# Converting float64 weights to float32 on the chip: a one-byte offset in the fetch, and four passes in another split over two engines

## The chip, the cores and the metric

The kernel runs on one core of a Trainium2 chip. The metric is the device time of one execution in microseconds (us). The core has five instruction streams: PE (TensorE, the matmuls; its weight loads are listed as PEld), DVE (VectorE), ACT (ScalarE), POOL (GpSimd) and SP (SyncE), which here only issues DMAs. Each stream runs its instructions in the order in which they were written and waits on semaphores for the others.

## The reference

The reference is an attention over 2 batches, 8 heads, 768 positions and head width 64, followed by two feed-forward layers on the 1536 x 512 result:

```python
scores = q @ k.T / 8 + bias(distance, head); scores masked to the last n_local and first n_global keys
x  = softmax(scores) @ v                      # float32, laid out as [1536, 512]
h  = x @ w_in;  x = (h * cos(h)) @ w_out      # w_in [512, 2048], w_out [2048, 512]
out = ((x @ w_a) * (x @ w_b)) @ w_out2        # w_a, w_b [512, 1536], w_out2 [1536, 512]
```

`q`, `k`, `v` are float32. The five weight matrices arrive as float64, and the chip's engines compute in float32, so the kernel turns the 64-bit words into float32 itself. A float64 word has a sign, 11 exponent bits and 52 mantissa bits; the float32 wanted has the same sign, 8 exponent bits and the upper 23 of the mantissa bits.

## The kernel before, in words

**Stages.** The attention comes first (`step`, the events table at the end of `tile_kernel`): twelve tiles of 128 queries, each cut into some forty steps (`TQ`, `S0`, `E0`, `T0`, `P0`, ...). A table gives each step a due time, and the steps are written in the order of those times; on PE, DVE, ACT and POOL that order is kept as written. Then comes `moe`: the first layer in three groups of 4, 6 and 6 blocks of 128 hidden columns, the second layer in six groups of 2 blocks. Each group goes over three chunks of 512 tokens. In this part only PE's order is kept as written; the order on the other engines is set by a scheduler when the program is built.

**A unit of the first layer** (`h_step`) is 12 matmuls into `h`, then on ACT a scaled copy `hs` (line 434), on DVE two passes that make the turns `u` (lines 435 and 436), on ACT the sine (line 440), on DVE the product (line 443), on ACT a rounded copy `gh` (line 455) and on POOL the rest `gl` (line 138). Pairs of `gh` and `gl` go into the 12 matmuls of `y` (lines 473 to 475), whose sum DVE adds to `yacc` (lines 477 and 479). Every matmul is done as three, with a rounded part and a rest of both operands.

**The weights** come in 68 blocks of 128 x 512 values, each 512 KB of float64. `load_block` fetches a block from SP's queue into a `raw` tile, of which there are two (the first six blocks go into the space of the accumulators). `conv_abs` and `conv_ops` make float32 of it: ACT takes the absolute value of the upper word as float32 (line 351, tile `cv`, two buffers), DVE clamps it (line 358), shifts it left by three (line 360), puts the sign and top exponent bit over it (line 361) and puts in three bits of the lower word (line 362). Then `conv_hi` rounds the block on ACT (`wh`, line 368) and `conv_lo` subtracts that on POOL (`wl`, line 138). Four blocks are converted during the attention, at the times of `CONV` and `OFF`; the others are converted in `moe`, where `fetch` writes each conversion ahead of the unit by whose turn it should be done.

Of the kernel before, what the change touches and what calls it, by code (L numbers as in the profile page):

```python
# [14 lines left out]
I32 = mybir.dt.int32  # L15
AF = mybir.ActivationFunctionType
# [3 lines left out]
P = 128  # L20
GLOB = 32
# [10 lines left out]
# When each step of a tile's attention is due, in tiles from the tile's own; the steps are written in the order of these.  # L32
# [3 lines left out]
OFF = (0.026, 0.448, 0.46, 1.374, 2.055, 2.1, 2.15)  # L36
# [11 lines left out]
def tile_kernel(ctx, tc, q, k, v, n_global, n_local, w_in, w_out, w_a, w_b, w_out2, out):  # L48
# [3 lines left out]
    DFF = w_in.shape[1]  # L52
    DF2 = w_a.shape[1]
# [33 lines left out]
    def read_counts():  # L87
        """The two int64 scalars as floats: high word (one more where the low word reads as negative) times 2^32, plus the low word."""
# [104 lines left out]
    def first_keys(i):  # L193
        """Keeps the first keys of a batch when its first tile has come."""
# [3 lines left out]
    def put_first_keys(i):  # L198
        """After the scores of tile i, the first keys of the batch take the place of its own first ones."""
# [3 lines left out]
    def split_v(i):  # L203
        """Three bfloat16 parts of V, the first with a column of ones beside it for the sum of the weights."""
# [92 lines left out]
    def first_values(i):  # L297
        """After the products of tile i with V, the first values of the batch take the place of its own first ones."""
# [28 lines left out]
    spare = [acc_pool.tile([P, 2, KD, 2 * P], I32, tag=f"acc{x}", name=f"raws{x}") for x in range(NCH)]  # L327

    def word_const(bits):
        return struct.unpack("<f", struct.pack("<I", bits))[0]  # L330

    def load_block(x):
        w, kind, idx = blocks[x]
        wi = w.bitcast(I32)
# [3 lines left out]
        else:  # L338
            raw = wp.tile([P, KD, 2 * P], I32, tag="raw", name=f"raw{x}", bufs=2)
        if kind == "col":  # L340
            nc.sync.dma_start(out=raw, in_=wi[:, idx * 2 * P:(idx + 1) * 2 * P].rearrange("(kk p) f -> p kk f", p=P))
        else:
            nc.sync.dma_start(out=raw, in_=wi[idx * P:(idx + 1) * P, :].rearrange("p (kk f) -> p kk f", kk=KD))
# [4 lines left out]
    def conv_abs(x):  # L348
        top = raws[x].rearrange("p k (f two) -> p k f two", two=2)[:, :, :, 1]
        cvs[x] = c = wp.tile([P, KD, P], I32, tag="cv", name=f"cv{x}", bufs=2)  # L350
        nc.scalar.activation(out=f(c), in_=f(top), func=AF.Abs)  # L351

    def conv_ops(x):
        pairs = raws.pop(x).rearrange("p k (f two) -> p k f two", two=2)
        low, top = pairs[:, :, :, 0], pairs[:, :, :, 1]
        c = cvs[x]
        return [
            lambda: nc.vector.tensor_scalar(out=f(c), in0=f(c), scalar1=word_const(896 << 20), scalar2=word_const((1151 << 20) - 1),  # L358
                                            op0=ALU.max, op1=ALU.min),
            lambda: nc.vector.tensor_scalar(out=c, in0=c, scalar1=3, scalar2=0x3FFFFFF8, op0=ALU.logical_shift_left, op1=ALU.bitwise_and),  # L360
            lambda: nc.vector.scalar_tensor_tensor(out=c, in0=top, scalar=-0x40000000, in1=c, op0=ALU.bitwise_and, op1=ALU.bitwise_or),  # L361
            lambda: nc.vector.scalar_tensor_tensor(out=c, in0=low, scalar=29, in1=c, op0=ALU.logical_shift_right, op1=ALU.bitwise_or)]  # L362
# [450 lines left out]
```

## Time and profile before

| | |
|---|---|
| timed runs | 732.21, 732.50, 733.02 us (median 732.5) |
| profiled execution, first to last instruction | 731.0 us |
| so around the span | 1.5 us |
| PE busy | 676.8 us (93%) |
| DVE busy | 510.7 us (70%) |
| ACT busy | 303.3 us (41%) |
| POOL busy | 289.8 us (40%) |
| DMA, all queues | 49.80 MB, 68 GB/s over the span |

The busy times are sums over stages that differ. The attention takes about the first 115 us, the first layer the next 300 and the second layer the rest. PE's busy time counts an instruction's whole stay in the pipeline, so the number of matmuls in a stretch tells more than the busy time. The granted clock is a share of 2.4 GHz.

### The profile page before, as it was taken

The page shows a single profiled execution, that of the slowest core. Times are in us where ns is not written, and L with a number is a line of the kernel's source. Part 1 is how long each engine was busy: PE and PEld are TensorE (multiplying, and loading weights), DVE is VectorE, ACT ScalarE, POOL GpSimd, SP SyncE. Part 2 cuts the span into 40 slices and gives each one's busy share as a digit, 9 for nine tenths or more (in the row PEclk, how much of TensorE's full clock was granted, in tenths as well). Part 3 has the DMA queues.
Part 4 walks back from the last instruction along what each step waited for, and adds up shares of the span by engine and source line. Part 5 has one row for each costly group of instructions (what it writes and reads, how often), then busy time and mean ns, then how long its engine had stood idle before and what let it go on. Part 6 is the DMA issues. An engine that isn't in the chain of part 4 may idle for free.

```text
span 731.0 us, 10359 instructions
## 1 busy us (share of the span) xinstructions
PE 676.8 (93%) x3936; PEld 556.5 (76%) x3936; DVE 510.7 (70%) x901; ACT 303.3 (41%) x559; POOL 289.8 (40%) x263
## 2 busy tenths in 40 slices
PE   4899998799885999999989698999999999999996
PEld 3778887588763788788878486888888888888885
DVE  6999898999999979859979715885727322222223
ACT  4798886554445444444454413334314111111110
POOL 5789851664444434425252404435315211111110
PEclk9999999989987799999999799999999999999998
DMA  9944320223333202201303101333301000000004
GB/s 210 249 108 107 81 48 1 86 71 103 98 103 115 87 30 87 87 1 58 105 11 109 64 0 31 106 114 95 117 1 57 1 1 0 1 1 0 1 29 150
DMA packets 65084, 49.80 MB, mean 68 GB/s; under 512 B 39168, under 2 KB 59648, under 8 KB 65024
## 3 DMA queue, kind: packets, MB, share of 16 engines
q1 hardware_dynamic: 65024, 49.04, 23.4%
q8 instruction: 33, 0.54, 0.3%
q14 instruction: 27, 0.22, 0.1%
HBM read 45.09 MB, written 3.15 MB: 66 GB/s over the span
## 4 chain that ended last, share of the span: by engine, by line
PE 50%; DVE 35%; ACT 6%; issue 4%; POOL 2%; DMA 2%; SPq 0%; POOLq 0%; ACTq 0%; DVEq 0%
DVE cv L361 6%; DVE u L436 5%; PE o L502 4%; PE o L503 4%; PE o L501 4%; DVE cv L362 4%; PE b L413 4%; PE b L412 4%; PE b L411 4%; PE a L412 4%; PE a L411 4%; PE a L413 4%; DVE u L435 4%; DVE cv L358 3%; DVE cv L360 3%
## 5 line engine op out<-in xcount | busy, mean ns | idle before, releaser
L138 POOL TENSOR_TENSOR wl<-cv,wh 128x512 fp32r<-128x512 f32 x68 | 97.1, 1431 | 167.1 <-ACT wh L368 163.9
L138 POOL TENSOR_TENSOR glu<-as,ghu 128x512 fp32r<-128x512 f32 x36 | 47.5, 1320 | 158.5 <-ACT ghu L455 158.5
L491 DVE TENSOR_TENSOR as<-b,as 128x512 f32<-128x512 f32 x36 | 24.8, 689 | 117.6 <-PE b L413 116.4
L138 POOL TENSOR_TENSOR gl<-u,gh 128x512 fp32r<-128x512 f32 x48 | 69.8, 1464 | 74.4 <-ACT gh L455 62.3
L411 PE MATMUL h<-xTh,wh 128*128 128x512 f32 x192 | 79.1, 412 | 7.6 <-ACT hs L434 5.8
L473 PE MATMUL y<-gh,wh 128*128 128x512 f32 x192 | 75.4, 393 | 9.2 <-ACT gh L455 9.2
L474 PE MATMUL y<-gl,wh 128*128 128x512 f32 x192 | 76.0, 396 | 6.4 <-POOL gl L138 6.4
L412 PE MATMUL h<-xTl,wh 128*128 128x512 f32 x192 | 79.0, 411 | 0.0
L413 PE MATMUL h<-xTh,wl 128*128 128x512 f32 x192 | 78.6, 409 | 0.0
L475 PE MATMUL y<-gh,wl 128*128 128x512 f32 x192 | 75.2, 392 | 0.0
L368 ACT ACTIVATE wh<-cv 128x512 fp32r<-128x512 f32 x68 | 42.7, 628 | 69.1 <-DVE cv L362 58.2
L440 ACT ACTIVATE u<-u,quarter 128x512 f32<-128x512 f32 x48 | 34.7, 723 | 72.1 <-DVE u L436 72.1
L507 DVE TENSOR_TENSOR oacc<-o,oacc 128x512 f32<-128x512 f32 x60 | 41.2, 690 | 31.6 <-PE o L503 31.6
L411 PE MATMUL a<-yh,wh 128*128 128x512 f32 x144 | 57.2, 398 | 6.3 <-ACT as L488 4.2
L411 PE MATMUL b<-yh,wh 128*128 128x512 f32 x144 | 57.6, 400 | 3.0 <-ACT hs L434 3.0
L488 ACT ACTIVATE as<-a 128x512 f32<-128x512 f32 x36 | 21.4, 593 | 88.6 <-PE a L413 88.6
L361 DVE SCALAR_TENSOR_TENSOR cv<-raw,cv 128x512 int32<-128x512 int32 x62 | 57.4, 926 | 0.9
L412 PE MATMUL a<-yl,wh 128*128 128x512 f32 x144 | 57.1, 396 | 0.6 <-DVE yl L482 0.6
L413 PE MATMUL b<-yh,wl 128*128 128x512 f32 x144 | 57.4, 398 | 0.0
L412 PE MATMUL b<-yl,wh 128*128 128x512 f32 x144 | 57.2, 398 | 0.0
L413 PE MATMUL a<-yh,wl 128*128 128x512 f32 x144 | 57.0, 396 | 0.0
L351 ACT ACTIVATE cv<-raw 128x512 f32<-128x512 f32 x62 | 41.4, 668 | 37.2 <-POOL wl L138 18.0
(106 smaller groups left out, 1540.7 us busy)
## 6 DMA issues: line engine op xcount, KB each, us to landing
raw<-in_moe_w_out_dram SPq DMA_DIRECT2D x26, 512.0 KB, 3.3
raw<-in_moe_w_in_dram SPq DMA_DIRECT2D x12, 512.0 KB, 3.7
raw<-in_moe_w_a_dram SPq DMA_DIRECT2D x12, 512.0 KB, 3.6
raw<-in_moe_w_b_dram SPq DMA_DIRECT2D x12, 512.0 KB, 3.6
nv<-in_v_dram SPq DMA_DIRECT2D x12, 256.0 KB, 4.3
out_dram<-oacc SPq DMA_DIRECT2D x12, 256.0 KB, 2.9
nq<-in_q_dram SPq DMA_DIRECT2D x11, 256.0 KB, 3.6
nk<-in_k_dram SPq DMA_DIRECT2D x11, 256.0 KB, 4.4
```

Of the source, the lines that this page charges most:

```text
L138: nc.gpsimd.tensor_tensor(out=dst, in0=a, in1=b, op=ALU.subtract)
L351: nc.scalar.activation(out=f(c), in_=f(top), func=AF.Abs)
L361: lambda: nc.vector.scalar_tensor_tensor(out=c, in0=top, scalar=-0x40000000, in1=c, op0=ALU.bitwise_and, op1=ALU.bitwise_or),
L368: nc.scalar.activation(out=hi, in_=f(cvs[x]), func=AF.Copy)
L411: nc.tensor.matmul(dst, wh[:, kk, :], xh[:, kk, :], start=(kk == 0), stop=False)
L412: nc.tensor.matmul(dst, wh[:, kk, :], xl[:, kk, :], start=False, stop=False)
L413: nc.tensor.matmul(dst, wl[:, kk, :], xh[:, kk, :], start=False, stop=(kk == KD - 1))
L436: nc.vector.scalar_tensor_tensor(out=u, in0=u, scalar=MAGIC, in1=hs, op0=ALU.subtract, op1=ALU.subtract)
L473: nc.tensor.matmul(yps, wh[:, m, :], gh, start=(x == 0), stop=False)
L474: nc.tensor.matmul(yps, wh[:, m, :], gl, start=False, stop=False)
L475: nc.tensor.matmul(yps, wl[:, m, :], gh, start=False, stop=(x == len(items) - 1))
L507: nc.vector.tensor_tensor(out=acc[:, u, :], in0=ops, in1=acc[:, u, :], op=ALU.add)
```

## The change

The host lays `w_in`, `w_a` and `w_b` out by blocks, so that each block is one piece of memory with 4 KB for each partition; the values and bytes stay the same. Every block is now fetched as bytes to an address one byte further on in the `raw` tile. The tile's 32-bit words are then no longer the lower and upper halves of a value: the word that is read holds the lower four exponent bits and the upper mantissa bits, and the byte with the sign and the upper seven exponent bits is read by itself, as a signed byte. ACT makes two float32 tiles of that byte, `cv` = relu(2^27 byte - 56 2^27) and `cn` = relu(-2^27 byte - 56 2^27), where `low_end` holds the second term, one value for each partition. DVE subtracts the two and writes the difference as an integer, which has the sign and the top exponent bits in place; a second DVE pass shifts the word right by five and puts it in. `cn` has one buffer. The second and third columns of times in `OFF` are now those of the two DVE passes; those of the former third and fourth passes are gone. The changes not shown remove docstrings and two unused names.

```diff
 P = 128
+RAW_BYTES = 8 * 4 * P + 32
+TOP = float(2.0**27)
-OFF = (0.026, 0.448, 0.46, 1.374, 2.055, 2.1, 2.15)
+OFF = (0.026, 0.448, 0.46, 2.1, 2.15)
...
-    spare = [acc_pool.tile([P, 2, KD, 2 * P], I32, tag=f"acc{x}", name=f"raws{x}") for x in range(NCH)]
+    spare = [acc_pool.tile([P, 2, RAW_BYTES], U8, tag=f"acc{x}", name=f"raws{x}") for x in range(NCH)]
+    low_end = const.tile([P, 1], F32, tag="lowend", name="low_end")
+    nc.gpsimd.memset(low_end, -56.0 * TOP)
...
-            raw = wp.tile([P, KD, 2 * P], I32, tag="raw", name=f"raw{x}", bufs=2)
-        if kind == "col":
-            nc.sync.dma_start(out=raw, in_=wi[:, idx * 2 * P:(idx + 1) * 2 * P].rearrange("(kk p) f -> p kk f", p=P))
-        else:
-            nc.sync.dma_start(out=raw, in_=wi[idx * P:(idx + 1) * P, :].rearrange("p (kk f) -> p kk f", kk=KD))
+            raw = wp.tile([P, RAW_BYTES], U8, tag="raw", name=f"raw{x}", bufs=2)
+        block = w[idx] if kind == "col" else w[idx * P:(idx + 1) * P, :]
+        nc.sync.dma_start(out=raw[:, 1:1 + 8 * KD * P], in_=block.bitcast(U8))
...
     def conv_abs(x):
-        top = raws[x].rearrange("p k (f two) -> p k f two", two=2)[:, :, :, 1]
-        cvs[x] = c = wp.tile([P, KD, P], I32, tag="cv", name=f"cv{x}", bufs=2)
-        nc.scalar.activation(out=f(c), in_=f(top), func=AF.Abs)
+        top = raws[x].bitcast(I8)[:, 8:8 + 8 * KD * P].rearrange("p (k f e) -> p k f e", k=KD, e=8)[:, :, :, 0]
+        cvs[x] = c, n = [wp.tile([P, KD, P], F32, tag=t, name=f"{t}{x}", bufs=b) for t, b in (("cv", 2), ("cn", 1))]
+        nc.scalar.activation(out=c, in_=top, func=AF.Relu, bias=low_end, scale=TOP)
+        nc.scalar.activation(out=n, in_=top, func=AF.Relu, bias=low_end, scale=-TOP)
 
     def conv_ops(x):
-        pairs = raws.pop(x).rearrange("p k (f two) -> p k f two", two=2)
-        low, top = pairs[:, :, :, 0], pairs[:, :, :, 1]
-        c = cvs[x]
+        words = raws.pop(x).bitcast(I32)[:, 0:2 * KD * P].rearrange("p (k f two) -> p k f two", k=KD, two=2)[:, :, :, 1]
+        c, n = cvs[x]
+        ci = c.bitcast(I32)
         return [
-            lambda: nc.vector.tensor_scalar(out=f(c), in0=f(c), scalar1=word_const(896 << 20), scalar2=word_const((1151 << 20) - 1),
-                                            op0=ALU.max, op1=ALU.min),
-            lambda: nc.vector.tensor_scalar(out=c, in0=c, scalar1=3, scalar2=0x3FFFFFF8, op0=ALU.logical_shift_left, op1=ALU.bitwise_and),
-            lambda: nc.vector.scalar_tensor_tensor(out=c, in0=top, scalar=-0x40000000, in1=c, op0=ALU.bitwise_and, op1=ALU.bitwise_or),
-            lambda: nc.vector.scalar_tensor_tensor(out=c, in0=low, scalar=29, in1=c, op0=ALU.logical_shift_right, op1=ALU.bitwise_or)]
+            lambda: nc.vector.tensor_tensor(out=ci, in0=c, in1=n, op=ALU.subtract),
+            lambda: nc.vector.scalar_tensor_tensor(out=ci, in0=words, scalar=5, in1=ci, op0=ALU.logical_shift_right, op1=ALU.bitwise_or)]
...
-        for y, fn in enumerate((conv_abs, conv_op, conv_op, conv_op, conv_op, conv_hi, conv_lo)):
+        for y, fn in enumerate((conv_abs, conv_op, conv_op, conv_hi, conv_lo)):
...
-        a = _np.ascontiguousarray(inputs[name])
+        a = inputs[name]
+        if name in ("moe_w_in", "moe2_w_a", "moe2_w_b"):
+            a = a.reshape(a.shape[0] // P, P, a.shape[1] // P, P).transpose(2, 1, 0, 3)
+        a = _np.ascontiguousarray(a)
```

The change also moves instructions, since the scheduler orders the engines other than PE anew. On DVE, around the second unit of the first layer's second group (`u0_1_1`; `cv19` is the tile of weight block 19), stood before:

```order
L443 SCALAR_TENSOR_TENSOR u0_1_0_3144<-hs0_1_0_3143,u0_1_0_3144 128x512
L358 TENSOR_SCALAR cv19_3082<-cv19_3082 128x512
L360 TENSOR_SCALAR cv19_3082<-cv19_3082 128x512
L361 SCALAR_TENSOR_TENSOR cv19_3082<-raw19_3017,cv19_3082 128x512
L435 TENSOR_SCALAR u0_1_1_3194<-hs0_1_1_3193 128x512
L362 SCALAR_TENSOR_TENSOR cv19_3082<-raw19_3017,cv19_3082 128x512
L436 SCALAR_TENSOR_TENSOR u0_1_1_3194<-u0_1_1_3194,hs0_1_1_3193 128x512
L477 COPY yacc1_3065<-y1_0_3_3204 128x512
L358 TENSOR_SCALAR cv20_3170<-cv20_3170 128x512
L443 SCALAR_TENSOR_TENSOR u0_1_1_3194<-hs0_1_1_3193,u0_1_1_3194 128x512
```

Now the same unit on DVE reads:

```order
L440 SCALAR_TENSOR_TENSOR u0_1_0_3146<-hs0_1_0_3145,u0_1_0_3146 128x512
L358 TENSOR_TENSOR cv20_3172<-cv20_3172,cn20_3173 128x512
L359 SCALAR_TENSOR_TENSOR cv20_3172<-raw20_3021,cv20_3172 128x512
L358 TENSOR_TENSOR cv21_3222<-cv21_3222,cn21_3223 128x512
L359 SCALAR_TENSOR_TENSOR cv21_3222<-raw21_3082,cv21_3222 128x512
L432 TENSOR_SCALAR u0_1_1_3196<-hs0_1_1_3195 128x512
L433 SCALAR_TENSOR_TENSOR u0_1_1_3196<-u0_1_1_3196,hs0_1_1_3195 128x512
L474 COPY yacc1_3067<-y1_0_3_3206 128x512
L440 SCALAR_TENSOR_TENSOR u0_1_1_3196<-hs0_1_1_3195,u0_1_1_3196 128x512
```

Blocks 20 and 21 now stand whole ahead of this unit, where block 19 was in work before. On ACT, around the same unit's `hs0_1_1`, stood before:

```order
L440 ACTIVATE u0_1_0_3144<-u0_1_0_3144,quarter_94 128x512
L351 ACTIVATE cv19_3082<-raw19_3017 128x512
L368 ACTIVATE wh18_3037<-cv18_3031 128x512
L434 ACTIVATE hs0_1_1_3193<-h0_1_1_3180 128x512
L455 ACTIVATE gh0_1_0_3150<-u0_1_0_3144 128x512
L368 ACTIVATE wh19_3088<-cv19_3082 128x512
```

Now ACT has there:

```order
L437 ACTIVATE u0_1_0_3146<-u0_1_0_3146,quarter_94 128x512
L351 ACTIVATE cn20_3173<-raw20_3021,low_end_112 128x512
L350 ACTIVATE cv21_3222<-raw21_3082,low_end_112 128x512
L351 ACTIVATE cn21_3223<-raw21_3082,low_end_112 128x512
L365 ACTIVATE wh20_3178<-cv20_3172 128x512
L431 ACTIVATE hs0_1_1_3195<-h0_1_1_3182 128x512
L452 ACTIVATE gh0_1_0_3152<-u0_1_0_3146 128x512
L365 ACTIVATE wh21_3228<-cv21_3222 128x512
L437 ACTIVATE u0_1_1_3196<-u0_1_1_3196,quarter_94 128x512
```

`hs0_1_1` now stands behind the passes of two blocks; `cn21` needs the one `cn` buffer, which DVE's subtraction for block 20 gives back. In the attention the two DVE passes of a block stand at the places of the former first two; for block 0 the place of the former third and fourth passes was this:

```order
L191 TENSOR_TENSOR kx_81<-tk1_0_203,kx_81 128x512
L361 SCALAR_TENSOR_TENSOR cv0_227<-raws0_109,cv0_227 128x512
L266 TENSOR_TENSOR pt0_0_1_243<-tp0_0_1_242,pt0_0_1_243 128x2x128
L362 SCALAR_TENSOR_TENSOR cv0_227<-raws0_109,cv0_227 128x512
L684 TENSOR_TENSOR su_104<-su_104 128x256
```

In the attention the rest of the order on DVE is as it was, with the `cv` rows of the third and fourth passes taken out.

## Rows read from the trace of the kernel before

**Rows 1.** Chain of work that ended last, shares of the span by engine and line
```profile
PE 50%; DVE 35%; ACT 6%; issue 4%; POOL 2%; DMA 2%; SPq 0%; POOLq 0%; ACTq 0%; DVEq 0%
DVE cv L361 6%; DVE u L436 5%; PE o L502 4%; PE o L503 4%; PE o L501 4%; DVE cv L362 4%; PE b L413 4%; PE b L412 4%; PE b L411 4%; PE a L412 4%; PE a L411 4%; PE a L413 4%; DVE u L435 4%; DVE cv L358 3%; DVE cv L360 3%
```

**Rows 2.** Stretches: us; PE, PEld, DVE, ACT, POOL busy (instructions); clock; DMA share; GB/s
```profile
15.00:60.00 45.00, 38.66 (x561) 32.86 (x562) 44.55 (x134) 34.29 (x77) 36.27 (x42) 1.00 0.70 174
115.00:246.00 131.00, 110.27 (x427) 86.95 (x427) 128.07 (x176) 65.52 (x109) 63.48 (x43) 0.88 0.27 85
246.00:300.00 54.00, 54.00 (x240) 44.70 (x239) 48.29 (x63) 25.22 (x43) 22.11 (x17) 1.00 0.22 69
300.00:402.00 102.00, 99.48 (x437) 81.53 (x436) 83.95 (x115) 45.06 (x76) 38.73 (x28) 1.00 0.20 61
402.00:450.00 48.00, 40.39 (x158) 32.05 (x156) 22.75 (x31) 15.21 (x26) 15.08 (x12) 0.89 0.08 25
450.00:727.00 277.00, 272.12 (x1191) 224.69 (x1191) 123.86 (x184) 63.35 (x104) 69.50 (x53) 0.99 0.14 46
```

**Rows 3.** PE's waits, 115 to 246 us: total us, times, longest us
```profile
PE y L473 <- ACT gh L455: 8.0, 3, 3.5
PE h L411 <- ACT hs L434: 5.8, 2, 3.0
PE y L474 <- POOL gl L138: 5.1, 4, 1.9
PE h L411 <- DVE xTl L320: 1.9, 1, 1.9
```

**Rows 4.** DVE in the first layer: start us, duration us, product of each unit
```profile
221.20 0.68 DVE L443 SCALAR_TENSOR_TENSOR u<-hs,u 128x512 f32<-128x512 f32 x1
...
228.43 0.68 DVE L443 SCALAR_TENSOR_TENSOR u<-hs,u 128x512 f32<-128x512 f32 x1
...
235.74 1.23 DVE L443 SCALAR_TENSOR_TENSOR u<-hs,u 128x512 f32<-128x512 f32 x1 [0.19 <-ACT u L440]
```

**Rows 5.** Tile cv alone: us; DVE, ACT, POOL busy (instructions); clock; DMA share; GB/s
```profile
15.00:60.00 45.00, 10.15 (x11) 3.27 (x5) 4.15 (x3) 1.00 0.70 174
115.00:246.00 131.00, 76.08 (x96) 30.80 (x49) 35.37 (x24) 0.88 0.27 85
```

**Rows 6.** Tile cv: count, shortest/median/longest ns, first and last start, forms
```profile
L358 DVE TENSOR_SCALAR cv<-cv x68: 411/422/1521, 13.6 to 562.6; 128x512 f32<-128x512 f32 x68
L360 DVE TENSOR_SCALAR cv<-cv x68: 408/427/1511, 14.0 to 563.5; 128x512 int32<-128x512 int32 x68
L368 ACT ACTIVATE wh<-cv x68: 612/632/637, 18.6 to 566.4; 128x512 fp32r<-128x512 f32 x68
...
L351 ACT ACTIVATE cv<-raw x62: 643/668/694, 123.2 to 561.1; 128x512 f32<-128x512 f32 x62
L361 DVE SCALAR_TENSOR_TENSOR cv<-raw,cv x62: 675/691/1807, 126.9 to 564.0; 128x512 int32<-128x512 int32 x62
L362 DVE SCALAR_TENSOR_TENSOR cv<-raw,cv x62: 675/684/1779, 127.8 to 564.7; 128x512 int32<-128x512 int32 x62
```

**Rows 7.** Groups by line and form: busy us, mean ns, idle before
```profile
L361 DVE SCALAR_TENSOR_TENSOR cv<-raw,cv 128x512 int32<-128x512 int32 x62 | 57.4, 926 | 0.9
L362 DVE SCALAR_TENSOR_TENSOR cv<-raw,cv 128x512 int32<-128x512 int32 x62 | 53.2, 858 | 0.8
...
L440 ACT ACTIVATE u<-u,quarter 128x512 f32<-128x512 f32 x48 | 34.7, 723 | 72.1 <-DVE u L436 72.1
```

**Rows 8.** PE's waits, 402 to 455 us: total us, times, longest us
```profile
PE a L411 <- ACT as L488: 4.2, 1, 4.2
PE b L411 <- ACT hs L434: 3.0, 1, 3.0
```

**Rows 9.** DMA issues: count, KB each, median us to landing
```profile
raw<-in_moe_w_out_dram SPq DMA_DIRECT2D x26, 512.0 KB, 3.3
raw<-in_moe_w_in_dram SPq DMA_DIRECT2D x12, 512.0 KB, 3.7
...
nk<-in_k_dram SPq DMA_DIRECT2D x11, 256.0 KB, 4.4
```

More of the change, by code (lines that the diff above doesn't have):

```diff
@@ L1 @@
 import math
-import struct
 from contextlib import ExitStack
@@ L15 @@
 I32 = mybir.dt.int32
+U8 = mybir.dt.uint8
+I8 = mybir.dt.int8
 AF = mybir.ActivationFunctionType
@@ L51, in tile_kernel @@
     NT, DM = out.shape
-    DFF = w_in.shape[1]
-    DF2 = w_a.shape[1]
     KD = DM // P
@@ L326, in tile_kernel @@
     seen = set()
-    spare = [acc_pool.tile([P, 2, KD, 2 * P], I32, tag=f"acc{x}", name=f"raws{x}") for x in range(NCH)]
-    def word_const(bits):
-        return struct.unpack("<f", struct.pack("<I", bits))[0]
+    spare = [acc_pool.tile([P, 2, RAW_BYTES], U8, tag=f"acc{x}", name=f"raws{x}") for x in range(NCH)]
+    low_end = const.tile([P, 1], F32, tag="lowend", name="low_end")
+    nc.gpsimd.memset(low_end, -56.0 * TOP)
     def load_block(x):
         w, kind, idx = blocks[x]
-        wi = w.bitcast(I32)
         if x < 2 * NCH and x not in seen:
@@ L367, in conv_hi @@
         lo = pool.tile([P, KD, P], F32R, tag="wl", name=f"wl{x}", bufs=bufs)
-        nc.scalar.activation(out=hi, in_=f(cvs[x]), func=AF.Copy)
+        nc.scalar.activation(out=hi, in_=cvs[x][0], func=AF.Copy)
         ready[x] = (hi, lo)
@@ L372, in conv_lo @@
         hi, lo = ready[x]
-        pool_sub(lo, f(cvs.pop(x)), f(hi))
+        pool_sub(lo, cvs.pop(x)[0], f(hi))
     def convert_block(x):
```

## The prediction

> **What bounds the kernel now.** I read the chain of waits first: VectorE (DVE) holds 35% of it, and the four passes of the weight conversion, lines 358, 360, 361 and 362, are 3 + 3 + 6 + 4 = 16% of the span [rows 1]. A share of a chain is no saving, so I went to the table of stretches [rows 2]. From 246 to 300 us TensorE (PE) does 240 matmuls in 54.0 us at the full clock: 0.225 us for each, PE's own pace. Against that pace 115 to 246 us needs 427 x 0.225 = 96.1 us and takes 131, so 34.9 us are lost; 300 to 402 loses 102 - 437 x 0.225 = 3.7; 402 to 450 loses 48 - 35.6 = 12.4; 450 to 727 loses 277 - 268 = 9.0. The largest loss lies where DVE is busy for 128.07 of 131 us, while ScalarE (ACT) has 65.52 and GpSimd (POOL) 63.48 [rows 2]. PE there waits for `gh`, `hs` and `gl`, 20.8 us in four kinds of wait [rows 3], and each comes from a queue that waits for DVE. The granted clock averages 0.88 in that stretch: the matmuls after such a pause run at 1.2 GHz before 2.4 comes back, which is the rest of the loss. At its worst a unit takes (235.74 - 221.20) / 2 = 7.27 us [rows 4], against 24 x 0.225 = 5.4 us of matmuls. In the attention, 15 to 60 us is a second stretch with a full DVE, 44.55 of 45 us; PE has 38.66 [rows 2].
>
> **What the change takes from DVE.** From 115 to 246 us DVE makes 96 passes on `cv`, 24 blocks, in 76.08 us, 3.17 us a block [rows 5]. The medians of the four passes sum to 0.422 + 0.427 + 0.691 + 0.684 = 2.22 us; the longest ones are 1.5 to 1.8 [rows 6], so about 0.95 us a block is waiting inside the instruction. The trace has a POOL subtraction of each block beside these passes, 35.37 us in the same stretch [rows 5], and I take that for what they wait for.
>
> The new block has a subtraction of two tiles and a shift with an or. The second is the form of line 362. The first, float32 in and integers out, stands nowhere in the trace: its bounds are 0.42, the pass over one tile, and 1.38 us, two passes of the kind of line 361 [rows 6]; I take line 361, the nearest in form, since it too reads two tiles. So a block costs 0.691 + 0.684 = 1.375 us undisturbed, or 0.926 + 0.858 = 1.784 at the means [rows 7]. If the collisions all stay, the relief is 24 x (2.22 - 1.375) = 20.3 us; if they go with the passes, 76.08 - 24 x 1.784 = 33.3 us. Both ends are below the 34.9 that PE lost, so PE's own pace is not reached before DVE's relief is used up.
>
> **What it adds to ACT.** One pass of 0.668 us becomes two with a bias for each partition. Such a pass stands in the trace as the sine, 0.723 us [rows 7]; the read with gaps costs 0.668 - 0.632 = 0.036 over a plain copy [rows 6]; together 0.76, with bounds of 0.63 (the copy) and, since no row reads bytes, 1.34 (twice the present pass). At 0.76 that is 2 x 0.76 - 0.668 = 0.85 us a block, and 24 x 0.85 = 20.4 us in the stretch: ACT goes from 65.5 to 86 us of busy time, which has room in 131 us, and in 111 too. At 1.34 it would be 65.5 + 24 x 2.01 = 114, and ACT's case below would hold.
>
> Room is not all, since ACT works in order. The second new pass waits for the single `cn` buffer, which DVE's subtraction for the block before gives back; behind it stand `wh` and `hs0_1_1`, as the new order of ACT shows, and `hs` is what DVE's next unit and a free `h` bank for PE wait for. So a unit with two blocks becomes a round through both queues: on DVE the product (0.69), the subtraction and the or (1.375), then, once `hs` is there, the first two passes of the next unit (0.42 + 0.69, medians of rows 6 for the same forms), on ACT `wh` and `hs` (0.63 each) and the sine (0.72). That is 5.16 us, and with one collision (1.8 - 0.69 = 1.1) 6.3 us. Against 7.27 it is 13% less, or 17 us of 131.
>
> Three estimates of the gain from 115 to 246 us: 17 by the round, 20.3 and 33.3 by DVE's work. I take 20, near the two lower ones.
>
> The Trainium skill speaks against moving this work at all: in ScalarE: Activation LUTs, Rules for kernel authors, relu, max and min belong on VectorE and not on ScalarE, being up to three times faster there (it says so of bf16). The trace agrees as far as it goes, 0.42 us for the clamp on DVE against 0.67 us for an ACT pass [rows 6]. By that rule nothing is won, 0.85 us off DVE for 0.85 us onto ACT in a block; it decides if ACT becomes the engine that is waited for, the first of the other ways below.
>
> **The attention.** From 15 to 60 us DVE makes 11 conversion passes, 2.75 blocks, in 10.15 us [rows 5]. At 1.375 to 1.784 us a block the relief is between 2.75 x 0.85 = 2.3 and 10.15 - 2.75 x 1.784 = 5.2 us; DVE is full there, so it shows. ACT gets 2.75 x 0.85 = 2.3 us on 34.29 of 45, which hides it. I take 3 us. What is late next is PE, at 38.66 of 45.
>
> **Elsewhere.** From 246 to 402 us DVE is relieved as well, but PE already loses only 3.7 us. From 402 to 450 us it loses 12.4 us with DVE at 22.75 of 48 [rows 2]: PE waits for ACT's `as` and `hs` in the change from the first to the second layer [rows 8], a chain that goes back and forth between engines, in which a conversion loses 0.85 us on DVE and gains 0.85 on ACT. I count it at 0, with 6 us either way. POOL's `wl` and ACT's `wh` stay as they are.
>
> **The fetch.** A block lands 3.3 to 3.7 us after its issue [rows 9]. Blocks from `w_in`, `w_a` and `w_b` come in longer pieces than before, so 3.3 is the lower bound. A write to an odd address has no row. The dearest row nearby is the load of `k`, 256 KB in 4.4 us [rows 9], so twice that, 8.8 us, bounds a block from above. I take the near end, 3.5: the size and the queue are those of the 3.3 row. The issue stays one DMA a block, in the background with DMA at 27% [rows 2].
>
> **Sum.** 731.0 - 20 - 3 = 708.0 us of span. The timed median, 732.5, lies 1.5 us over the span of the profiled execution; with that, 709.5 us.
>
> **The other ways.**
>
> ACT takes over. For it: each of its waits lies in the same round, and the new one comes on top. Against it: DVE's backlog is what most of its idle time waits for. If half of the 65.5 us in which ACT now stands idle stays, the stretch needs 86 + 33 = 119 us, a gain of 12; with 2 in the attention and 1 lost at the change of layers, 719.5 us. Chance 0.17.
>
> The whole loss comes back. For it: conversions stand earlier in the new order (blocks 20 and 21 done ahead of the unit that had block 19), so the second half of the stretch finds them made. The relief of 30, 4 in the attention, and 6 of the 12.4 us at the change of layers make 40: 692.5 us. Chance 0.19.
>
> The conversion becomes no cheaper. With the subtraction at 1.38 us and the collisions kept, 0.16 us a block is left of the 0.85, 4 us; the longer ACT round eats it: 732 us. Chance 0.03.
>
> Slower: odd addresses make the fetch the bound. With two `raw` buffers, a buffer's round is the landing, two ACT passes (1.5) and two DVE passes (1.4). A block is needed every 131 / 24 = 5.5 us, a buffer every 10.9, so it decides from a landing of 8.0 us on. At 8.8 a block takes 5.85 us, the stretch 140, 9 more than now. The first eight blocks come while the attention loads its tiles with DMA at 70% [rows 2]: 8 x 5.5 us more, less the idle 30% of 45 us, is 30 us late. Sum about 770 us. Against it: nothing in the trace; for it: nothing either, hence a chance of 0.06.
>
> **How the numbers follow.** My forecast, 709.5, has 0.55, with its own range of 699 to 716. The range over the cases runs from 690, which takes in most of the full recovery, to 726, which takes in ACT as the bound; outside lie the fetch, the dear conversion and the tails. 0.2% is 1.5 us, about what a measurement of this kernel can tell from no change. Faster by more: 0.55 + 0.17 + 0.19, less 0.01 for a tail of ACT's case, 0.90. Within: 0.03. Slower: the fetch at 0.06 and 0.01 of that tail, 0.07.
>
> **What would show it.** Right: `cv` has two DVE passes of some 0.69 us at the median, from 115 to 240 us DVE falls below 90% busy, the number of matmuls in 20 us rises to about 80, the waits for `gh` and `hs` shrink, and ACT has 20 us more work there. The attention ends some 3 us sooner. ACT's case would show as PE waiting for `hs` behind `cn` waits with DVE idle. Wrong altogether: landings of `raw` over 8 us, or a subtraction over 1.3 us at the median.

## The result, and the profile after

The changed kernel takes **715.0 us** (median of 4 runs, 713.97 to 716.69) against 732.76 (4 runs, 732.21 to 733.1) of the kernel before: ratio 0.9751, 95% interval 0.9734 to 0.9768, a gain of 17.8 us. Its profiled execution is 712.9 us, 18.1 less than the 731.0 of before. The forecast was 709.5 us, a gain of 23.

The lines that answer to the rows of before have other numbers now: the two relus are 350 (`cv`) and 351 (`cn`), DVE's subtraction is 358 and its shift with or 359, `wh` is 365, POOL's subtractions are 139, `hs` is 431, the product is 440, `gh` is 452. The chain of waits, shares by engine and by line [rows 1]:

```profile
PE 61%; DVE 18%; ACT 8%; POOL 5%; issue 5%; DMA 2%; DVEq 0%; POOLq 0%; ACTq 0%; SPq 0%
PE o L500 5%; PE o L499 5%; PE o L498 5%; PE b L408 4%; PE b L409 4%; PE b L410 4%; PE a L409 4%; PE a L410 4%; PE a L408 4%; DVE cv L358 3%; DVE cv L359 3%; DVE u L433 3%; DVE u L432 3%; PE o L281 3%; PE y L471 3%
```

DVE has halved its share, the conversion's 16% are 6. The same stretches as in [rows 2], with the same columns (us; PE, PEld, DVE, ACT, POOL busy; clock; DMA share; GB/s):

```profile
15.00:60.00 45.00, 39.63 (x553) 33.51 (x552) 41.56 (x127) 36.05 (x82) 34.12 (x42) 0.96 0.66 169
115.00:246.00 131.00, 118.17 (x483) 94.63 (x482) 114.08 (x142) 88.58 (x144) 65.44 (x45) 0.93 0.30 97
246.00:300.00 54.00, 54.00 (x240) 44.66 (x239) 40.87 (x50) 29.96 (x50) 23.39 (x17) 1.00 0.19 59
402.00:450.00 48.00, 44.62 (x182) 35.97 (x181) 19.36 (x23) 16.60 (x27) 14.00 (x11) 0.93 0.14 44
```

In 115 to 246 us PE does 483 matmuls where it did 427; DVE is 87% busy, ACT has 23 us more. PE's waits there, total us, times and longest [rows 3]:

```profile
PE y L471 <- POOL gl L139: 4.1, 3, 2.0
PE h L408 <- ACT hs L431: 3.7, 2, 3.2
PE h L408 <- DVE xTl L321: 3.6, 1, 3.6
PE y L470 <- ACT gh L452: 1.5, 2, 1.1
```

The waits for `gh` and `hs` went from 13.8 to 5.2 us, all four kinds together from 20.8 to 12.9. DVE, which before waited 1.8 us in all from 113 to 246 us, now waits 16.3, most of it for `cn`:

```profile
DVE cv L358 <- ACT cn L351: 9.2, 11, 2.1
```

Tile `cv` alone, DVE, ACT and POOL busy [rows 5], and its durations, with those of `cn` (shortest/median/longest ns) [rows 6]:

```profile
15.00:60.00 45.00, 4.29 (x5) 3.44 (x5) 3.29 (x3) 0.96 0.66 169
115.00:246.00 131.00, 53.67 (x53) 34.38 (x50) 36.69 (x25) 0.93 0.30 97
```

```profile
L358 DVE TENSOR_TENSOR cv<-cv,cn x68: 674/693/1787, 13.6 to 545.0; 128x512 int32<-128x512 f32 x68
...
L350 ACT ACTIVATE cv<-raw,low_end x62: 741/758/780, 121.0 to 543.3; 128x512 f32<-128x512 int8 x62
L359 DVE SCALAR_TENSOR_TENSOR cv<-raw,cv x62: 674/693/1784, 125.8 to 545.7; 128x512 int32<-128x512 int32 x62
```

```profile
L351 ACT ACTIVATE cn<-raw,low_end x62: 730/750/785, 123.2 to 544.0; 128x512 f32<-128x512 int8 x62
```

The means, with busy time, mean ns and the idle time before [rows 7], and the landings of the blocks [rows 9]:

```profile
L358 DVE TENSOR_TENSOR cv<-cv,cn 128x512 int32<-128x512 f32 x68 | 65.7, 966 | 29.1 <-ACT cn L351 25.0
...
L359 DVE SCALAR_TENSOR_TENSOR cv<-raw,cv 128x512 int32<-128x512 int32 x62 | 61.5, 993 | 1.2
```

```profile
raw<-in_moe_w_out_dram SPq DMA_DIRECT2D x26, 512.0 KB, 3.3
raw<-in_moe_w_in_dram SPq DMA_DIRECT2D x12, 512.0 KB, 3.3
```

Over the whole run, the DVE passes on `cv` beside which no two-input pass of POOL runs (67) take 674 to 782 ns, and the other passes on `cv` (69) take 1255 ns on average. So POOL is what the passes wait for, as the prediction took it.

**Where the time went.** PE does the same 2448 matmuls of 128x512 in the two layers, in the same order. Counted by their starts in the trace, these are the stretches of work (us), here and in the runs told of below. "First" is the start of the first of them, a matmul of `h`; "to 432" is the time from there until 432 of them have started, and so on; "last" is the last of the 2448. Each ratio is to the kernel before as it was timed together with that run:

| run | first | to 432 | to 1080 | to 1296 | to last | median of runs (n), ratio to before [95%] |
|---|---|---|---|---|---|---|
| before | 113.59 | 133.5 | 150.3 | 65.8 | 260.9 | 732.76 (4) |
| changed | 113.42 | 120.9 | 147.9 | 63.9 | 260.9 | 715.0 (4), 0.9751 [0.9734, 0.9768] |
| before, two passes less | 112.32 | 119.8 | 147.5 | 62.1 | 260.9 | 711.25 (5), 0.9688 [0.9671, 0.9706] |
| changed, no `cn` pass | 112.19 | 119.7 | 147.8 | 62.3 | 260.9 | 710.83 (5), 0.9689 [0.9676, 0.9702] |
| changed, whole-word address | 112.27 | 122.7 | 147.9 | 63.8 | 260.9 | 715.0 (5), 0.973 [0.9713, 0.9747] |
| changed, blocks 0 to 3 free | 108.69 | 120.0 | 147.9 | 64.0 | 260.9 | 709.84 (5), 0.9675 [0.9659, 0.9691] |
| `wl` of block 0 later | 111.05 | 122.7 | 147.9 | 63.9 | 260.9 | 714.92 (5), 0.9746 [0.9723, 0.977] |
| blocks 0 to 2 later | 119.99 | 123.6 | 149.8 | 63.3 | 265.2 | 730.25 (8), 0.9964 [0.9943, 0.9984] |
| two `cn` buffers | 112.49 | 122.7 | 147.9 | 61.7 | 260.9 | 714.15 (5), 0.9744 [0.9722, 0.9766] |
| no subtraction | 110.52 | 112.4 | 148.4 | 63.9 | 260.9 | 705.36 (5), 0.9628 [0.9604, 0.9652] |
| subtraction on POOL | 112.36 | 136.7 | 154.6 | 66.2 | 260.9 | 738.42 (5), 1.0079 [1.0066, 1.0092] |

So of the 18.1 us between the profiled executions the attention gave 0.2, the first layer 12.6 up to matmul 432 and 2.4 more up to 1080, the change of layers 2.0, and 1.0 came behind the last matmul.

### The profile page after: what moved, and what is told of

Read it like the earlier page. It is cut to its first block, busy times and chain, and to the rows that moved or that the text cites. A ratio compares the mean times of both kernels' runs of the same rounds, so it can differ in the third digit from the quotient of the medians.

```text
span 712.9 us, 10352 instructions
## 1 busy us (share of the span) xinstructions
PE 670.9 (94%) x3936; PEld 553.9 (78%) x3936; DVE 448.4 (63%) x765; ACT 352.1 (49%) x627; POOL 287.9 (40%) x264
## 3 DMA queue, kind: packets, MB, share of 16 engines
q1 hardware_dynamic: 49664, 49.04, 22.9%
## 4 chain that ended last, share of the span: by engine, by line
PE 61%; DVE 18%; ACT 8%; POOL 5%; issue 5%; DMA 2%; DVEq 0%; POOLq 0%; ACTq 0%; SPq 0%
PE o L500 5%; PE o L499 5%; PE o L498 5%; PE b L408 4%; PE b L409 4%; PE b L410 4%; PE a L409 4%; PE a L410 4%; PE a L408 4%; DVE cv L358 3%; DVE cv L359 3%; DVE u L433 3%; DVE u L432 3%; PE o L281 3%; PE y L471 3%
## 5 line engine op out<-in xcount | busy, mean ns | idle before, releaser
L139 POOL TENSOR_TENSOR gl<-u,gh 128x512 fp32r<-128x512 f32 x48 | 68.2, 1429 | 72.2 <-ACT gh L452 62.1
L358 DVE TENSOR_TENSOR cv<-cv,cn 128x512 int32<-128x512 f32 x68 | 65.7, 966 | 29.1 <-ACT cn L351 25.0
L409 PE MATMUL h<-xTl,wh 128*128 128x512 f32 x192 | 77.5, 403 | 0.0
L350 ACT ACTIVATE cv<-raw,low_end 128x512 f32<-128x512 int8 x62 | 47.1, 759 | 31.1 <-POOL wl L139 18.3
L359 DVE SCALAR_TENSOR_TENSOR cv<-raw,cv 128x512 int32<-128x512 int32 x62 | 61.5, 993 | 1.2
```

Source lines behind the costliest of these rows:

```text
L139: nc.gpsimd.tensor_tensor(out=dst, in0=a, in1=b, op=ALU.subtract)
L350: nc.scalar.activation(out=c, in_=top, func=AF.Relu, bias=low_end, scale=TOP)
L358: lambda: nc.vector.tensor_tensor(out=ci, in0=c, in1=n, op=ALU.subtract),
L359: lambda: nc.vector.scalar_tensor_tensor(out=ci, in0=words, scalar=5, in1=ci, op0=ALU.logical_shift_right, op1=ALU.bitwise_or)]
L409: nc.tensor.matmul(dst, wh[:, kk, :], xl[:, kk, :], start=False, stop=False)
```

## The experiments

**Two DVE passes less, and nothing else.** The kernel before, with lines 358 and 360 left out:

```diff
-            lambda: nc.vector.tensor_scalar(out=f(c), in0=f(c), scalar1=word_const(896 << 20), ...
-            lambda: nc.vector.tensor_scalar(out=c, in0=c, scalar1=3, scalar2=0x3FFFFFF8, ...
```

> The kernel before (aligned fetch, rows as they were, one ACT pass per block) without the clamp and the shift on VectorE (lines 358 and 360): two DVE passes per block are left, of the two-input kind, as in the changed kernel; the clamp and the shift are not computed, so the weights are other numbers. Theory (VectorE's relief is the cause, and ACT's added pass costs a little): 708 to 714 us, at or a few us below the changed kernel's 715. Rival (ACT's added pass costs what my ACT case said, about half of the relief): 700 to 705. Rival (the gain came from the fetch or the layout, fewer packets): 730 to 733. First h matmul at 113 us in the first two, since the attention gained nothing.

It took 711.25 us, where the theory had it; the ratio, 0.9688, makes the gain 22.9 us of 732.76, the medians 21.5. Old fetch, old layout, one ACT pass: the relief of DVE by itself gives the whole gain and more, and the fetch and the layout are out as its cause. The first matmul of `h` came at 112.32 us, so the attention does gain by it, 1.3 us, against what I expected.

**The changed kernel without the second ACT pass.**

```diff
-        nc.scalar.activation(out=n, in_=top, func=AF.Relu, bias=low_end, scale=-TOP)
```

> The changed kernel without the second ACT pass (cn is not made; DVE subtracts cv from itself, so the sign and top exponent bits of the weights are missing). DVE's work stays, ACT loses 0.75 us per block. Theory (ACT's pass lies mostly beside other work, but 24 DVE passes waited 25 us on it): 711 to 714 us. Rival (ACT's pass costs nothing at all): 715, within 1. Rival (ACT holds half of the relief back): 700 to 707.

It took 710.83 us, at the lower end of the theory, and agrees with the run before it stretch by stretch (table). So ACT's added work costs 4.2 us by the medians: 1.2 in the attention, 1.2 up to matmul 432, 0.1 to 1080 and 1.6 at the change of layers. DVE still stands idle for 14.1 us of 115 to 246 us there, with no `cn` to wait for.

**A whole-word address.**

```diff
-        nc.sync.dma_start(out=raw[:, 1:1 + 8 * KD * P], in_=block.bitcast(U8))
+        nc.sync.dma_start(out=raw[:, 4:4 + 8 * KD * P], in_=block.bitcast(U8))
...
-        top = raws[x].bitcast(I8)[:, 8:8 + 8 * KD * P].rearrange("p (k f e) -> p k f e", k=KD, e=8)[:, :, :, 0]
+        top = raws[x].bitcast(I8)[:, 4:4 + 8 * KD * P].rearrange("p (k f e) -> p k f e", k=KD, e=8)[:, :, :, 7]
...
-        words = raws.pop(x).bitcast(I32)[:, 0:2 * KD * P].rearrange("p (k f two) -> p k f two", k=KD, two=2)[:, :, :, 1]
+        words = raws.pop(x).bitcast(I32)[:, 1:1 + 2 * KD * P].rearrange("p (k f two) -> p k f two", k=KD, two=2)[:, :, :, 1]
```

> The changed kernel with the blocks fetched to an address four bytes on instead of one, the sign byte read from its new place, and the second DVE pass reading the word one on, which is then the upper half of a value (so the exponents are other numbers); counts, shapes and strides of all passes stay. Theory (the odd address costs nothing): 715 us, within 1, raw landings 3.3 us. Rival (the odd address costs in the fetch or in the strided byte read): 2 to 10 us faster, landings below 3.2 us or ACT passes below 0.75.

715.0 us, landings of 3.2 to 3.3 us, the relu of `cv` 762 ns at the median against 758: the odd address costs nothing that these runs show.

**No `cn` and no DVE passes in the attention.** Blocks 0 to 3 keep the first ACT pass, `wh` and `wl`:

```diff
-        nc.scalar.activation(out=c, in_=top, func=AF.Relu, bias=low_end, scale=TOP)
+        nc.scalar.activation(out=c, in_=top, func=AF.Relu, bias=low_end, scale=TOP if x >= 4 else 1.0)
...
+        if x < 4:
+            return [lambda: None, lambda: None]
```

> The changed kernel with the conversion of blocks 0 to 3, the ones in the attention, reduced to one ACT pass (no cn, no DVE passes; these four blocks become zeros). Theory (PE and the splitting on POOL pace the attention, VectorE does not): first h matmul at 113.4 us as now, total within 1 of 715. Rival (the two ACT passes at 22 us cost what the four removed DVE passes gave): first h matmul at 111 to 112, total 713. Rival of the prediction (each conversion pass in 15 to 60 us moves the end by itself): 110, total 711.

The first matmul of `h` came at 108.69 us, 4.7 sooner, the total at 709.84. The theory was wrong, and the rivals too small: the passes left out here cost 4.7 us in the changed kernel. All of it lies before the first tile's `xTh` (29.50 us against 34.27), and from there on the distance stays within a microsecond. So I looked at 17 to 24 us. DVE's pass over `su`, which goes into the bias, and the last pass of the bias (start, duration), in the kernel before and in the changed one:

```profile
18.95 0.24 DVE L685 TENSOR_SCALAR su<-su,counts 128x32 f32<-128x32 f32 x1
...
19.64 1.39 DVE L665 TENSOR_TENSOR bias<-bias,su 128x256 f32<-128x256 f32 x1
```

```profile
17.68 2.20 DVE L682 TENSOR_SCALAR su<-su,counts 128x32 f32<-128x32 f32 x1
...
20.61 1.30 DVE L662 TENSOR_TENSOR bias<-bias,su 128x256 f32<-128x256 f32 x1
```

What POOL did then, first before, then in the changed kernel (`nq` is a product, `wl` a subtraction):

```profile
16.56 1.46 POOL L162 TENSOR_TENSOR nq<-nq,qf 128x512 f32<-128x512 f32 x1
19.32 1.43 POOL L138 TENSOR_TENSOR wl<-cv,wh 128x512 fp32r<-128x512 f32 x1 [1.29 <-ACT wh L368]
```

```profile
17.27 1.27 POOL L163 TENSOR_TENSOR nq<-nq,qf 128x512 f32<-128x512 f32 x1
18.51 1.25 POOL L139 TENSOR_TENSOR wl<-cv,wh 128x512 fp32r<-128x512 f32 x1
```

Before, POOL stood idle from 18.02 to 19.32, waiting for the slow conversion, and the pass over `su` fell into the gap. The cheaper conversion closed the gap: `wl` follows `nq` at once, and the pass ends at 19.88, 0.1 us after `wl`. The kernel before had not escaped, though: there `wl` stood beside the last pass of the bias, 1.39 us, and the bias was copied at 21.06, only 0.9 us sooner than now. Nor is the pass over `su` the whole of the 4.7 us, since it took 2.12 us in the run just told of too. Behind the last pass of the bias ACT's copy of it waits, and behind that the two relus of block 1 stand ahead of the exponentials (line 250):

```profile
21.94 0.51 ACT L686 ACTIVATE bias<-bias 128x128 f32<-128x128 f32 x2 [4.26 <-DVE bias L662]
22.36 0.75 ACT L350 ACTIVATE cv<-raws,low_end 128x512 f32<-128x512 int8 x1
23.02 0.77 ACT L351 ACTIVATE cn<-raws,low_end 128x512 f32<-128x512 int8 x1
23.68 0.90 ACT L250 ACTIVATE sp<-sp,mm 128x256 f32<-128x256 f32 x2
```

The Trainium skill has such a stop in SBUF — State Buffer, Who interferes with whom: VectorE in its two-port modes needs the pair of ports that it shares with GpSimd, and whichever issues first holds it for a whole instruction, the other standing still. The trace agrees on the standing still, and no run shows the mode of this pass; but here the pass stood through two POOL instructions, 2.20 us. The first of them alone would have made it 1.1, an estimate: from 17.68 until that one's end at 18.54, and 0.24.

The first tile loses something else that the kernel before did not: PE's clock falls to 1.2 GHz at 30 us. The stretch 28 to 32 us of the changed kernel, and of the run with the whole-word address (columns as in [rows 2]):

```profile
28.00:32.00 4.00, 3.38 (x22) 2.58 (x23) 3.77 (x13) 2.86 (x7) 3.50 (x4) 0.75 0.49 177
```

```profile
28.00:32.00 4.00, 3.34 (x35) 2.39 (x34) 3.97 (x13) 3.15 (x7) 3.83 (x4) 1.00 0.53 205
```

In the whole-word run the bias is copied 0.4 us later (22.34 us) and the two relus stand there as well, and still the first `xTh` comes at 33.45, 0.8 us sooner. The runs with two DVE passes less and without the `cn` pass have the fall too, the other runs that keep both relus do not.

**`wl` of block 0 six microseconds later**, to test POOL's part:

```diff
-            events.append((at_ + by * OFF[y], "conv", fn, x))
+            events.append((at_ + by * OFF[y] + (0.5 if x == 0 and y == 4 else 0), "conv", fn, x))
```

> The changed kernel with one instruction moved: block 0's rest (wl on POOL, line 139, at 18.5 us) is written after the third tile's values and queries on POOL, some 6 us later. In the changed kernel VectorE's pass over su (128x32, line 682) took 2.20 us beside it, 0.24 in the kernel before, where POOL stood idle then. Theory (VectorE's short pass is held until POOL's subtractions in a row have ended, and the cheaper conversion brought wl up behind nq into that place): line 682 takes 1.2 us or less, the bias is ready 1 to 2 us sooner, the first tile's xTh comes at 32.3 to 33.3 us instead of 34.3, the total at 713 to 714. Rival (the two ACT passes in front of the exponentials are what the attention lost, and the pass over su is beside the path): su's pass shorter but xTh at 34.2, total 715. Rival (not POOL): line 682 still 2.2 us.

The pass over `su`, the last pass of the bias, and POOL beside them:

```profile
18.76 0.24 DVE L682 TENSOR_SCALAR su<-su,counts 128x32 f32<-128x32 f32 x1
...
19.45 0.43 DVE L662 TENSOR_TENSOR bias<-bias,su 128x256 f32<-128x256 f32 x1
```

```profile
16.48 1.46 POOL L163 TENSOR_TENSOR nq<-nq,qf 128x512 f32<-128x512 f32 x1
17.89 0.10 POOL L209 MEMSET vx<- 128x16 bf16 x1
19.70 0.66 POOL L142 TENSOR_SCALAR vx<-nv 128x512 bf16<-128x512 f32 x1 [1.71 <-DMA nv<-in_v_dram]
```

With POOL idle the pass is back at 0.24 us; the bias is copied at 19.91 instead of 21.94, `xTh` comes at 31.92 instead of 34.27, the first matmul of `h` at 111.05 instead of 113.42. The theory of POOL holds, but `su` is the smaller part: its pass ends 0.9 us sooner, and the two passes of the bias behind it, free of POOL as well, take 1.2 us less. Yet the total did not move (714.92): the first layer took 122.7 us to matmul 432 instead of 120.9, and 0.8 us more came behind the last matmul. The stretches 218 to 222, 222 to 226 and 226 to 230 us of the changed kernel, and of this one (columns as in [rows 2]):

```profile
218.00:222.00 4.00, 3.06 (x7) 2.48 (x8) 2.83 (x6) 2.78 (x6) 0.99 (x2) 0.50 0.41 131
222.00:226.00 4.00, 4.00 (x14) 3.11 (x13) 3.75 (x4) 2.25 (x4) 4.00 (x3) 0.68 0.00 0
226.00:230.00 4.00, 2.79 (x11) 1.79 (x10) 3.18 (x3) 2.93 (x5) 2.23 (x3) 1.00 0.26 88
```

```profile
218.00:222.00 4.00, 4.00 (x14) 3.15 (x13) 3.78 (x5) 3.02 (x6) 2.29 (x2) 0.68 0.01 2
222.00:226.00 4.00, 2.99 (x14) 2.14 (x12) 3.40 (x4) 2.59 (x5) 2.41 (x2) 1.00 0.00 0
226.00:230.00 4.00, 2.79 (x7) 2.03 (x7) 3.50 (x3) 1.65 (x4) 2.96 (x2) 0.67 0.42 133
```

PE, ahead, now stops twice: it waits 1.0 us for `gh` at 225.8, 1.2 us for `gl` at 227.5, and falls to 1.2 GHz a second time with that. Over 115 to 246 us the clock comes to 0.93 in both kernels; what differs are the waits, for `gh` 3.2 us in all instead of 1.5. A PE that comes earlier waits for the other engines there. The whole-word run and the one with two `cn` buffers show the same: first matmul 0.9 to 1.2 us sooner, 122.7 us to matmul 432. The run without conversion passes in the attention kept its lead (120.0): its clock came to 0.95 there, by which PE gains 2.6 us at most, an estimate; what kept the clock up is open.

**Blocks 0 to 2 converted later in the attention.**

```diff
-CONV = ((-0.4, 0.192), (0, 1.145), (2, 1), (11.427, 0.333))
+CONV = ((2.5, 1), (4.5, 1), (6.5, 1), (11.427, 0.333))
```

> The changed kernel with the conversions of blocks 0, 1 and 2 written at 2.5, 4.5 and 6.5 tiles instead of around 0, 0 and 2. Theory (the attention's first 35 us are the dear place, since the first tile's chain of bias and exponentials has nothing beside it; later, PE paces): first tile's xTh at 29.5 us, first h matmul at 109 to 111 us, total 711 to 713. Rival (VectorE is full everywhere in the attention, so that the passes cost the same wherever they stand): first h matmul at 113.4, total 715.

The first tile's `xTh` came at 30.30 us, as the theory had it, but the fifth at 69.45 against 66.81, the seventh at 88.07 against 81.25, and the total was 730.25. Both guesses fell: the place is dear everywhere, and dearer later, 6.6 us by the first matmul of `h`. That is less than half of the 15.3 us. Behind matmul 1296 the run lost 4.3 us more, where PE waits for nothing in either kernel and a matmul takes 0.230 us instead of 0.227 at the same clock; why is open. DVE at 64 us:

```profile
63.93 0.68 DVE L358 TENSOR_TENSOR cv<-cv,cn 128x512 int32<-128x512 f32 x1
64.65 1.49 DVE L359 SCALAR_TENSOR_TENSOR cv<-raws,cv 128x512 int32<-128x512 int32 x1
66.07 0.68 DVE L294 TENSOR_TENSOR xn<-o,rl 128x512 f32<-128x512 f32 x1
```

`xn` stands behind 2.1 us of conversion, and PE waited 1.7 us for it, ACT 2.5 for the maxima behind it.

**Two buffers of `cn`.**

```diff
-[wp.tile([P, KD, P], F32, tag=t, name=f"{t}{x}", bufs=b) for t, b in (("cv", 2), ("cn", 1))]
+[wp.tile([P, KD, P], d, tag=t, name=f"{t}{x}", bufs=2) for t, d in (("cv", F32), ("cn", BF16))]
```

> The changed kernel with cn in bfloat16 (its values fit) and two buffers of it in the space of one. DVE's subtraction waited 24 times, 25 us in all, for the second ACT pass, and the single cn made that pass wait for DVE's subtraction 5 times, 6.8 us. Theory (ACT's 4 us come from its time in front of hs and the exponentials, not from the buffer): 714 to 716. Rival (the single buffer ties ACT to DVE and holds PE): 711 to 713.

714.15 us, as the theory had it: the single buffer is not what ACT costs.

**No subtraction on DVE.** Both ACT passes stay, with a scale of 1 and -1:

```diff
-            lambda: nc.vector.tensor_tensor(out=ci, in0=c, in1=n, op=ALU.subtract),
```

> The changed kernel without the subtraction on DVE (line 358); both ACT passes stay, with a scale of 1, so that cv is zero and the weights nearly so. One DVE pass per block is left. Theory (VectorE still bounds the first layer at places, 87% busy in 113 to 246 us): another 0.97 us per block gives 3 to 8 us between the first h matmul and matmul 432, which took 120.9 us in the changed kernel, total 705 to 711 with what the attention gains. Rival (what is left of the loss is in the rounds of ACT, POOL and PE, and VectorE has stopped mattering): 120 to 121 us there, total 713 to 715.

705.36 us. The first layer took 112.4 us to matmul 432, 8.5 less, and 2.9 came from the attention. DVE's load still costs PE time in the first layer; the 8.5 are a little over what I had for it.

**The subtraction on POOL.** ACT writes `cv` and `cn` as 32-bit integers for it:

```diff
-            lambda: nc.vector.tensor_tensor(out=ci, in0=c, in1=n, op=ALU.subtract),
...
+        sub = nc.vector if x < 4 else nc.gpsimd
...
+            lambda: sub.tensor_tensor(out=c, in0=c, in1=n, op=ALU.subtract),
```

> The changed kernel with cv and cn written by ACT as 32-bit integers (same values), and from block 4 on the subtraction done by POOL instead of VectorE. The run without the subtraction gave 8.5 us between the first h matmul and matmul 432, so that much is there to be had; POOL was busy 65.4 us of 133 there and would do 24 passes more of 1.0 to 1.3 us, as its other 128x512 subtractions take. Theory (VectorE is the bound, POOL has room): 705 to 710 us, the first layer to matmul 432 in 113 to 117 us instead of 120.9. Rival (POOL's longer stays hold VectorE's passes and delay gl and wl, so that the relief is lost): 714 to 720.

738.42 us, slower than the kernel before, and further off than the rival said. DVE is relieved, and it does not help; the stretch, and the largest wait in 113 to 246 us:

```profile
115.00:246.00 131.00, 105.96 (x413) 84.16 (x412) 85.82 (x97) 78.86 (x128) 90.93 (x67) 0.88 0.26 88
```

```profile
DVE cv L359 <- POOL cv L358: 37.2, 18, 3.7
```

DVE works in order: the shift with or stands in its queue and waits for POOL, 37 us in all, and the products and turns of the units wait behind it. The Trainium skill says in Perfetto Trace Analysis, Optimizing Scalar/DVE Operations, that moving work to ScalarE may pay where VectorE is full, and that moving it between GpSimd and VectorE, which share a port, might not. Both halves agree with these runs: 21.5 us of relief for 4.2 by the one, 23.4 lost by the other. What the trace shows for the loss is the wait in DVE's queue; what the port adds no run takes apart.

**Three versions put together from these.** The subtraction on POOL with `wl` of block 0 later; two `cn` buffers with `wl` of block 0 later; and the latter with block 1's relus one instruction ahead of the copy of the bias, whose line is shown.

```diff
-            events.append((at_ + by * OFF[y], "conv", fn, x))
+            events.append((at_ + by * OFF[y] + {(0, 4): 0.5, (1, 0): -0.0087}.get((x, y), 0), "conv", fn, x))
```

> The same as the run with the subtraction on POOL, and block 0's rest on POOL written later, as in the run that moved it alone, where the attention ended 2.4 us sooner and the first layer gave 1.8 us of it back. Theory (the gain was given back because VectorE was full in the first layer; with room there it stays): 2 to 2.5 us faster than the run with the subtraction on POOL alone. Rival (the give-back has nothing to do with VectorE's load): equal to it within 1 us.

> The changed kernel with cn in bfloat16 and two buffers, and block 0's rest on POOL later; VectorE keeps both passes. Each alone gave about 1 us or nothing in total. Theory (the attention's 2.4 us are given back again, since VectorE stays as full): 712.5 to 715. Rival (the two add up): 710 to 712.

> The run with cn in bfloat16 and block 0's rest later, and in addition block 1's two ACT passes written one instruction ahead of the copy of the bias, where ACT stood idle 1.15 us, instead of behind it and ahead of the first tile's exponentials. Theory (these two passes are what ACT costs in the attention; the run without the second one gained 1.2 us there): xTh of the first tile 1.0 to 1.4 us before that of the run it is built on, first h matmul at 110.0 to 110.6 us; of that VectorE's load in the first layer takes back half or more, total 711.5 to 713. Rival (it stays whole): 710 to 711.5. Rival (the passes are no longer on the path): first h at 111.4, total 713.

They took 738.01 us (ratio 1.0083, 1.0064 to 1.0102), 712.97 (0.9736, 0.9723 to 0.975) and 713.43 (0.974, 0.9721 to 0.9759). The first lies 0.4 us from its base: the rival was right, though with DVE waiting for POOL this run says little of DVE's load in the changed kernel. The second had its first `h` at 111.44 and matmul 432 at 234.62, against 234.31 in the changed kernel: the lead was given back, as expected, and its 2 us under the changed kernel, from the change of layers (61.5 us instead of 63.9), lie within the intervals. In the third the first `xTh` came 0.75 us later than in the second, not sooner. There ACT waits for DVE's maxima:

```profile
18.21 0.74 ACT L351 ACTIVATE cn<-raws,low_end 128x512 bf16<-128x512 int8 x1
19.48 0.51 ACT L686 ACTIVATE bias<-bias 128x128 f32<-128x128 f32 x2 [0.52 <-DVE bias L662]
21.77 0.91 ACT L250 ACTIVATE sp<-sp,mm 128x256 f32<-128x256 f32 x2 [1.78 <-DVE mm L242]
```

With the bias early, the relus are no longer on the path: DVE's maxima wait 1.5 us for PE's scores, and PE waits 2.8 us for POOL's `nq` (line 163), which is late next. The second version has the same two waits, so what makes the third 0.75 us later than it is open. None of the versions is shown to be faster than the changed kernel.

## Why the prediction was right, and where it was not

- **The mechanism** was right: DVE's relief is the gain. Taking two passes out of the kernel before gave 21.5 us; the odd address cost nothing that the runs show.
- **The sizes of the passes.** Subtraction 0.691 forecast, 0.693 at the median; ACT 0.76 forecast, 0.758 and 0.750; landing 3.5 forecast, 3.3. The collisions went in part: 0.95 us a block before, 2.03 - 1.39 = 0.64 now in 115 to 246 us. The mean pair, 0.966 + 0.993 = 1.96 us, is dearer than the 1.784 of the upper estimate.
- **115 to 246 us, 20 us taken, 12.6 measured** up to matmul 432; this is the mis-sized term. DVE's passes on `cv` went from 3.17 to 53.67 / 26.5 = 2.03 us a block, so 24 blocks were relieved by 27 us, inside 20.3 to 33.3. But PE got only 12.6 / 27 = 0.47 us for each of them, and in the run without the subtraction 8.5 us for 24 x 0.966 = 23.2, or 0.37. The sum took PE's gain for DVE's relief. What PE did not get, DVE spends waiting: it stood idle for 131 - 128.07 = 2.9 us before and for 131 - 114.08 = 16.9 now. ACT's pass explains 1.2 of the 7.4 missing. For the rest PE waits for `gl`, `hs` and `xTl`; that these are late by other engines too is how I read the waits, and no run takes them one by one. The unit's round is neither confirmed nor refuted: four units from 209.59 us on take 24.1 us, 6.0 each with 6.3 forecast, but singly between 3.7 and 9.1. Nor was 7.27 us a unit at its worst: in the kernel before, products stand up to 9.0 us apart (189.7 to 198.7 us).

```profile
209.59 0.68 DVE L440 SCALAR_TENSOR_TENSOR u<-hs,u 128x512 f32<-128x512 f32 x1
...
233.72 0.91 DVE L440 SCALAR_TENSOR_TENSOR u<-hs,u 128x512 f32<-128x512 f32 x1 [0.79 <-ACT u L437]
```

- **The attention, 3 us taken, 0.2 measured.** "DVE is full there, so it shows" failed, and so did "which hides it" of ACT. DVE's passes on `cv` in 15 to 60 us shrank by 5.9 us, but DVE's busy time by 3.0, since others grew, that over `su` by 2.0. The first tile's `xTh` came at 34.27 us instead of 32.55: the bias is copied 0.9 later, one more relu (0.75) stands ahead of the exponentials, and PE's clock falls. By the fourth tile the changed kernel had made that up (59.43 against 59.15). Changed one at a time, `wl` written later is worth 2.4 us at the first matmul and no second relus 1.2. That the two add up is not shown, and a part of the 2.4 the kernel before paid too, so how the missing 2.8 us divide stays open.
- **Elsewhere, 0 taken, 2.4 + 2.0 + 1.0 measured**: 2.4 between matmuls 432 and 1080, 2.0 at the change of layers, inside its 6 either way, and 1.0 behind the last matmul. The sum had no cause for them. It is luck that they came out on the good side and made up for 5.4 of the 10.2 us that the two terms missed: 23 forecast, 17.8 measured, and 715.0 lies just inside the own range, which ends at 716.
- **ACT's case** was a price, not the bound: 4.2 us in all. The Trainium skill's rule on relu (ScalarE: Activation LUTs, Rules for kernel authors) puts it on VectorE and not on ScalarE. The runs do not agree with it here: 4.2 us paid for 21.5.
- **The signs.** DVE below 90% busy (87%), the waits for `gh` and `hs` shrunk, 20 us more on ACT (23): seen. 80 matmuls in 20 us: 483 / 131 x 20 = 74. The attention's 3 us: not seen.

## What to carry to other kernels

Time taken off the fullest engine comes back at a rate, here 0.37 to 0.47 us for each us, and the engine spends the rest waiting; measure that rate by leaving a pass out before pricing the whole relief. In queues that run in order, a cheaper step also moves what stands behind it, and the new neighbours can collide. A pass that goes to an engine with free time makes the full engine's queue wait for it: 9.2 us from 113 to 246 us for ACT's `cn`, which paid, and 37.2 for POOL's subtraction, which did not. Price that wait before the relief.

## What the runs showed of the hardware

- A DVE pass of 0.24 us (128x32) took 2.20 us beside two POOL passes in a row, a product and a subtraction, and ended 0.1 us after the second; in the run with two `cn` buffers, where only the second ran beside it, it took 1.18.
- In the changed kernel DVE's passes of 128x512 on `cv` take 0.67 to 0.78 us with no two-input pass of POOL beside them and 1.26 on average with one.
- POOL's subtraction of 128x512 integers takes 1.29 us at the median, DVE's 0.69.
- The granted clock in 115 to 246 us rose from 0.88 to 0.93, with 12.9 us of PE's waits instead of 20.8, and to 0.97 without the subtraction. (0.93 - 0.88) x 131 = 6.6 us is an estimate of what that gives PE at most, a part of the 12.6 that no pass's duration shows.
